# Moving the last step of a layer norm from ScalarE to GpSimd in a fused attention and feed-forward kernel

## The chip, the cores and the metric

One core of one Trainium2 chip. The metric is device time in microseconds (us). The engines are called PE (TensorE matmul), ACT (ScalarE), DVE (VectorE), POOL (GpSimd) and SP (SyncE, which here only issues transfers). SBUF and PSUM are two memories on the core: in this kernel PE's matmuls write to PSUM tiles (bank by bank), and the other tiles shown here lie in SBUF. A transfer from one memory to another is a DMA; it is issued by an engine's queue and lands some us later.

## The reference, cut to what matters

```python
# q, k, v: 8 batches, 12 heads, 448 tokens, 64 wide
scores = scale * np.matmul(q, k.transpose(0, 1, 3, 2))
attn = np.maximum(scores, 0.0) ** 2 / S
x = np.matmul(attn, v)                  # -> (8, 448, 768)
X = np.fft.fft(np.fft.fft(x, axis=1), axis=2)
u = x + np.real(X)
mu, var = u.mean(-1), u.var(-1)         # over the 768 channels
un = (u - mu) / np.sqrt(var + 1e-06)    # the layer norm
out = u + np.maximum(un @ w_ch1, 0.0) @ w_ch2
```

The last step of the norm is `un = u * rstd + nmr`, with `rstd` one over the root and `nmr = -mu * rstd`, both one number per token.

## The kernel before

A Python scheduler inside the kernel books every instruction on an engine with an estimated duration, and so decides the order of each engine's queue. On the chip each queue then runs in that order.

```python
def need(eng, dur, deps=(), bufs=(), ok=None):
    return eng, dur, list(deps), list(bufs), ok

def act(n):
    return n / 1200 + 0.2
```

The norm in `mix_rows`, once for each of two chunks of rows (`ch`) of a batch `b`; each chunk has two tiles `u`:

```python
for i, eng, en, d in ((1, nc.gpsimd, "POOL", 1.8), (0, nc.vector, "DVE", 2 * dve(KN))):
    ...                                            # u, half on POOL, half on DVE
    eng.tensor_tensor(u[:n, 0:KN], ts[i][:n, 0:KN], x[:n, 0:KN], op=ALU.add)
    eng.tensor_tensor(u[:n, KN:D], ts[1 - i][:n, KN - 2:0:-1], x[:n, KN:D], op=ALU.add)
...                                                # bn_stats, bn_aggr on DVE
nc.scalar.activation(std[:n], mv[:n, :, 1], AF.Sqrt, bias=eps_t[:n])
...
nc.vector.reciprocal(rstd[:n], std[:n])
nc.vector.scalar_tensor_tensor(nmr[:n], mv[:n, :, 0], -1.0, rstd[:n], op0=ALU.mult, op1=ALU.mult)
for i, u in enumerate(us):
    e = yield need("ACT", act(D), [e + (LATENCY["DVE"] if i == 0 else 0.0)])
    un = work.tile([128, D], BF16, name="un", tag=f"un{2 * ch + i}", bufs=1)
    nc.scalar.activation(un[:n], u[:n], AF.Identity, bias=nmr[:n, i:i + 1],
                         scale=rstd[:n, i:i + 1])
    ...
```

From batch 2 on, `un` then goes to memory (half by SP, half by a scattered store that POOL issues) and comes back transposed through SP as `unT` for the feed-forward. The feed-forward's first half fills PSUM banks that ACT empties; it has two banks for this (and DVE's work on attention outputs and on `o` uses the same two):

```python
BF = Banks(2, lambda i: psum.tile([128, 512], FP32, name="psF", tag=f"F{i}", bufs=1))
...
e = yield need(en, (dve if en == "DVE" else act)(N), [e + LATENCY["PE"]], [BH[j]])
nc.scalar.activation(h[:, 0:N], ph[:, 0:N], AF.Relu)      # hT
BF.give(ph, e)
```

## Time and profile before

| | before |
|---|---|
| time, median of 3 runs | 611.16 us (610.72 to 611.26) |
| profiled span | 610.0 us |
| busy: PE, DVE, ACT, POOL | 597.8, 331.7, 315.6, 126.8 us |
| PE's waits after 165 us | 1.1 us on ACT's `hT`, 0.5 us on DVE's `o` |

How to read it: PE is the bound, and the other engines matter only where PE waits for them. The prediction shows the lines. The tiles named most often: `sq` are the squared scores, `xT` the attention outputs on their way out of PSUM, `fold` sums made of `xT`, `qkr` the queries and keys as copied by DVE and `qkT` the same after a transposing transfer, `hT` the first half of the feed-forward after its relu, `o` the output rows, to which a reload brings `u` back from memory.

### The profile page before, as it was taken

The page shows a single profiled execution, that of the slowest core. Times are in us where ns is not written, and L with a number is a line of the kernel's source. Part 1 is how long each engine was busy: PE and PEld are TensorE (multiplying, and loading weights), DVE is VectorE, ACT ScalarE, POOL GpSimd, SP SyncE. Part 2 cuts the span into 40 slices and gives each one's busy share as a digit, 9 for nine tenths or more (in the row PEclk, how much of TensorE's full clock was granted, in tenths as well). Part 3 has the DMA queues.
Part 4 walks back from the last instruction along what each step waited for, and adds up shares of the span by engine and source line. Part 5 has one row for each costly group of instructions (what it writes and reads, how often), then busy time and mean ns, then how long its engine had stood idle before and what let it go on. Part 6 is the DMA issues. An engine that isn't in the chain of part 4 may idle for free.

```text
span 610.0 us, 10248 instructions
## 1 busy us (share of the span) xinstructions
PE 597.8 (98%) x4044; PEld 330.6 (54%) x4063; DVE 331.7 (54%) x767; ACT 315.6 (52%) x470; POOL 126.8 (21%) x175
## 2 busy tenths in 40 slices
PE   8998999999999999999999999999999999999997
PEld 6566556544455565555445565555445565554464
DVE  5966776965576768555744368545742447110011
ACT  5965772488555668536763167635782247114300
POOL 8432031411142124211420115210410004000000
PEclk9998999999999999999999999999999999999999
DMA  9999998965938995976496775985461225320022
GB/s 125 207 209 228 207 179 126 203 118 101 148 120 166 197 166 168 172 137 120 158 140 115 134 126 173 167 156 96 146 134 61 86 51 177 102 94 23 0 78 78
DMA packets 125216, 82.22 MB, mean 135 GB/s; under 512 B 76272, under 2 KB 113168, under 8 KB 125168
## 3 DMA queue, kind: packets, MB, share of 16 engines
q0 software_dynamic: 40320, 34.07, 35.3%
q1 hardware_dynamic: 84848, 47.50, 32.1%
q8 instruction: 32, 0.52, 0.3%
q14 instruction: 16, 0.13, 0.1%
HBM read 62.91 MB, written 26.69 MB: 147 GB/s over the span
## 4 chain that ended last, share of the span: by engine, by line
PE 84%; DVE 6%; ACT 5%; SPq 2%; issue 1%; DMA 1%; DVEq 0%; ACTq 0%
PE psF L1108 32%; PE psF L1090 31%; PE psF L524 7%; PE psS L538 6%; PE psS L982 2%; PE psS L1130 2%; ACT sq L558 2%; DVE stats L864 1%; PE psS L832 1%; ACT un L878 1%; SPq L923 1%; DMA o<-ubot 1%; PE psS L957 1%; PE psF L421 1%; ACT hT L1063 1%
## 5 line engine op out<-in xcount | busy, mean ns | idle before, releaser
L1090 PE MATMUL psF<-unT,w 128*128 128x384 bf16 (+1 forms) x1134 | 228.4, 353 | 2.2 <-ACT hT L1063 1.1
L558 ACT ACTIVATE sq<-psS 112x896 bf16<-112x896 f32 x192 | 165.3, 915 | 116.2 <-PE psS L538 116.2
L1108 PE MATMUL psF<-w,hT 128*128 128x384 bf16 (+2 forms) x1343 | 224.8, 326 | 0.1
L1108 PEld LDWEIGHTS <-hT 128*128 128x128 bf16 x1344 | 129.3, 98 | 92.4 <-issue 8.8
L1090 PEld LDWEIGHTS <-w 128*128 128x128 bf16 x1152 | 109.5, 98 | 111.6 <-issue 15.4
L1063 ACT ACTIVATE hT<-psF 128x512 bf16<-128x512 f32 (+1 forms) x180 | 98.2, 547 | 98.8 <-PE psF L1090 97.7
L564 DVE TENSOR_TENSOR sq<-sq 112x896 bf16<-112x896 bf16 x192 | 115.4, 619 | 48.5 <-ACT sq L558 46.9
L1071 DVE TENSOR_TENSOR o<-psF,o 128x384 f32<-128x384 f32 (+2 forms) x56 | 31.0, 554 | 109.8 <-PE psF L1108 108.5
L445 DVE TENSOR_SCALAR xT<-psF 128x224 bf16<-128x224 f32 x48 | 18.7, 390 | 74.7 <-PE psF L524 74.7
L538 PE MATMUL psS<-qkT 64*112 64x448 bf16 x384 | 52.6, 367 | 0.6 <-ACT qkT L426 0.4
L300 POOL DMA_DIRECT2D vn<-in_v_dram x24 | 17.3, 720 | 172.7 <-PE psF L524 154.1
L524 PE MATMUL psF<-sq,vn 112*64 112x448 bf16 x384 | 45.5, 358 | 1.4 <-DVE o L1071 0.5
L852 POOL TENSOR_TENSOR u<-tp,xn 128x385 f32<-128x385 f32 (+1 forms) x14 | 17.3, 1236 | 105.1 <-DVE tp L843 91.6
L538 PEld LDWEIGHTS <-qkT 64*112 64x112 bf16 x384 | 20.4, 125 | 27.9 <-issue 22.7
L878 ACT ACTIVATE un<-u,nmr,rstd 128x768 bf16<-128x768 f32 (+1 forms) x28 | 28.2, 1021 | 6.7 <-DVE nmr L873 6.7
L524 PEld LDWEIGHTS <-vn 112*64 112x64 bf16 x384 | 18.3, 109 | 23.1 <-issue 14.5
L864 DVE BATCH_NORM_STATS2 stats<-u 128x6 f32<-128x384 f32 (+1 forms) x56 | 28.1, 540 | 0.0
L900 POOL DMA_INDIRECT ubot<-u,back x16 | 16.8, 1048 | 43.3 <-DVE sq L564 27.5
L1130 PE MATMUL psS<-warm 128*128 128x126 bf16 (+1 forms) x210 | 18.9, 242 | 1.3 <-DVE warm L215 1.3
L300 POOL DMA_DIRECT2D qn<-in_q_dram x21 | 15.3, 728 | 23.1 <-DVE sq L564 9.2
L900 POOL DMA_INDIRECT nbot<-un,back x12 | 11.7, 972 | 35.6 <-ACT un L878 31.9
L452 DVE TENSOR_SCALAR xT<-psF 128x224 bf16<-128x224 f32 x47 | 18.0, 384 | 0.0
(119 smaller groups left out, 363.5 us busy)
## 6 DMA issues: line engine op xcount, KB each, us to landing
out_dram<-o SPq DMA_DIRECT2D x27, 384.0 KB, 2.6
vn<-in_v_dram POOLq DMA_DIRECT2D x24, 224.0 KB, 4.5
qn<-in_q_dram POOLq DMA_DIRECT2D x21, 224.0 KB, 6.3
kn<-in_k_dram POOLq DMA_DIRECT2D x21, 224.0 KB, 6.9
w<-in_moe_w_ch_dram POOLq DMA_DIRECT2D x12, 384.0 KB, 13.5
w<-in_moe_w_ch_dram POOLq DMA_DIRECT2D x4, 1152.0 KB, 23.4
utop<-u SPq DMA_DIRECT2D x8, 384.0 KB, 2.6
o<-utop SPq DMA_DIRECT2D x8, 384.0 KB, 3.5
```

The costliest lines, as they stand in the source:

```text
L300: nc.gpsimd.dma_start(out=t, in_=src[b, hs].rearrange("h (p j) d -> p h (j d)", j=4))
L524: nc.tensor.matmul(av[h * Dh:(h + 1) * Dh, 0:S], lhsT=vn[:, c, h0 + h, :], rhs=sq[:, h, :], start=(c == 0), stop=(c == 3))
L538: nc.tensor.matmul(sc[:R, h, 0:S].rearrange("k (c q) -> k c q", c=4), lhsT=kT[ps, m % 2, c, :], rhs=qT[ps, m % 2], start=True, stop=True)
L558: nc.scalar.activation(r, sc[:R, :, 0:S], AF.Relu)
L564: nc.vector.tensor_tensor(r, r, r, op=ALU.mult)
L864: nc.vector.bn_stats(stats[:n, hf, :], u[:n, hf * (D // 2):(hf + 1) * (D // 2)])
L878: nc.scalar.activation(un[:n], u[:n], AF.Identity, bias=nmr[:n, i:i + 1], scale=rstd[:n, i:i + 1])
L1063: nc.scalar.activation(h[:, 0:N], ph[:, 0:N], AF.Relu)
L1071: nc.vector.tensor_tensor(o[:, hs], pc[:, 0:w], o[:, hs], op=ALU.add)
L1090: nc.tensor.matmul(ph[:, 0:N], lhsT=w1_sb[m][hf][:, jj * 128:(jj + 1) * 128], rhs=unT[:, m, 0:N], start=(m == 0), stop=(m == MC - 1))
L1108: nc.tensor.matmul(pc[:, 0:w], lhsT=hT[j][:, c * 128:(c + 1) * 128], rhs=w2_sb[j // 6][:, j % 6, hs], start=(j == 0), stop=(j == JC - 1))
L1130: nc.tensor.matmul(first_pps[0][:, t, c0:512], lhsT=warm[:, 0:128], rhs=warm[:, c0:512], start=not begun, stop=False)
```

## The change

The intent is to relieve ACT, which also empties PSUM for PE, by giving 24 of its instructions to POOL, which is idle for four fifths of the time. Both the instruction and the scheduler's booking change.

```diff
         for i, u in enumerate(us):
-            e = yield need("ACT", act(D), [e + (LATENCY["DVE"] if i == 0 else 0.0)])
+
+            en = "POOL" if b > 1 else "ACT"
+            e = yield need(en, act(D) if b == 1 else 1.05, [e + (LATENCY["DVE"] if i == 0 else 0.0)])
             un = work.tile([128, D], BF16, name="un", tag=f"un{2 * ch + i}", bufs=1)
-            nc.scalar.activation(un[:n], u[:n], AF.Identity, bias=nmr[:n, i:i + 1],
-                                 scale=rstd[:n, i:i + 1])
+            if b > 1:
+                nc.gpsimd.tensor_scalar(un[:n], u[:n], rstd[:n, i:i + 1], nmr[:n, i:i + 1],
+                                        op0=ALU.mult, op1=ALU.add)
+            else:
+                nc.scalar.activation(un[:n], u[:n], AF.Identity, bias=nmr[:n, i:i + 1],
+                                     scale=rstd[:n, i:i + 1])
```

## The prediction

> **What bounds the kernel now.** I read the busy table of the page first, then the six stretches between 165 us (where batch 2's norm begins) and 545 us (where the last layer's own stretch begins), then who TensorE (PE) waited for in that part, and then the order of time around one norm.
>
> The busy table, from the page; the columns are engine, busy us, share of the span, instructions:
>
> ```profile
> PE 597.8 (98%) x4044; PEld 330.6 (54%) x4063; DVE 331.7 (54%) x767; ACT 315.6 (52%) x470; POOL 126.8 (21%) x175
> ```
>
> PE is busy for 98% of the span; ScalarE (ACT), which the change relieves, for 52%, and POOL for 21%. A busy PE can still be a slow one, so the next thing is how much of it is idle where the change acts. The busy times by stretch (stretch, its length, then busy us of each engine, the granted clock last but two):
>
> ```profile
> 165.00:230.00 65.00, 64.42 (x432) 36.25 (x431) 44.87 (x102) 36.84 (x53) 17.30 (x19) 1.00 0.88 164
> 230.00:305.00 75.00, 74.35 (x461) 38.45 (x463) 48.75 (x116) 46.26 (x71) 19.94 (x23) 1.00 0.72 150
> 305.00:370.00 65.00, 64.95 (x417) 36.20 (x417) 32.07 (x74) 29.98 (x45) 10.66 (x13) 1.00 0.71 126
> 370.00:445.00 75.00, 74.74 (x462) 38.66 (x465) 47.29 (x113) 46.00 (x71) 17.65 (x20) 1.00 0.65 148
> 445.00:510.00 65.00, 64.95 (x417) 36.52 (x417) 29.36 (x66) 28.24 (x43) 4.20 (x4) 1.00 0.33 85
> 510.00:545.00 35.00, 34.26 (x208) 20.31 (x208) 8.61 (x19) 8.79 (x17) 4.94 (x5) 1.00 0.39 120
> ```
>
> The PE column adds up to 377.66 of 380 us: 2.3 us of idle PE in the whole part in which a norm has moved. The clock is 1.00 throughout. PE is also fast while busy: inside the feed-forward, matmul follows matmul every 162 to 163 ns for 384 columns and 216 ns for 512 (start to start), the same in every stretch. So PE's own program is the bound. The waits of PE from 165 us on (who, for whom, us in total, times, longest) are two rows:
>
> ```profile
> PE psF L1090 <- ACT hT L1063: 1.1, 3, 0.5
> PE psF L524 <- DVE o L1071: 0.5, 1, 0.5
> ```
>
> The first is the one that the change can take away, and the order of time around batch 7's norm shows why (start, duration, engine, line, operation, and in brackets the idle time before it and what ended that):
>
> ```profile
> 510.37 0.91 POOL L852 TENSOR_TENSOR u<-tp,xn 112x385 f32<-112x385 f32 x1 [1.31 <-DVE rstd L871]
> 510.38 0.91 DVE L873 SCALAR_TENSOR_TENSOR nmr<-mv,rstd 128x2 f32<-128x2 f32 x1
> 511.22 0.55 DVE L852 TENSOR_TENSOR u<-tm,xn 112x385 f32<-112x385 f32 x1
> 511.24 1.22 POOL L853 TENSOR_TENSOR u<-tm,xn 112x383 f32<-112x383 f32 x1
> 511.33 1.03 ACT L878 ACTIVATE un<-u,nmr,rstd 128x768 bf16<-128x768 f32 x1 [0.50 <-DVE nmr L873]
> 511.69 1.19 DVE L853 TENSOR_TENSOR u<-tp,xn 112x383 f32<-112x383 f32 x1
> 512.27 0.85 ACT L1063 ACTIVATE hT<-psF 128x384 bf16<-128x384 f32 x2
> 512.79 6.09 PE L1090 MATMUL psF<-unT,w 128*128 128x384 bf16 x36 [0.53 <-ACT hT L1063]
> ```
>
> ACT begins the norm step `un` at 511.33, and the relu `hT`, which empties one of the two PSUM banks that PE needs, only comes after it, at 512.27. PE stands for 0.53 us. The three such stalls are near 237 (batch 4), 512 and 519 us (batch 7).
>
> **What the Trainium skill says.** "SBUF — State Buffer", section "Who interferes with whom": GpSimd shares a port pair with VectorE (DVE), and "A DVE instruction with two SBUF inputs contends with a GpSimd instruction that reads SBUF". The trace agrees: above, `nmr` (128 by 2) takes 0.91 us, exactly as long as the POOL addition that starts 0.01 us before it, where its median over all 14 is 0.161 us. "GPSIMD Engine Reference", section 3.1, puts the per-element cost of a simple one-input body between about 1.03 and 1.8 cycles at 1.2 GHz, which for 768 elements is an estimate of 0.66 to 1.15 us; this trace has the very operation at 0.981 us (below), and that is used. "Perfetto Trace Analysis", section "Identifying Performance Opportunities", says that improving a kernel generally means improving its most-contended engine; here that is PE, and the change does not touch PE's work.
>
> **The change part by part.** The two rows of the grouped instructions that give the cost (line, engine, operation, shapes, count, then busy us and mean ns of one, then idle before and releaser):
>
> ```profile
> L878 ACT ACTIVATE un<-u,nmr,rstd 128x768 bf16<-128x768 f32 (+1 forms) x28 | 28.2, 1021 | 6.7 <-DVE nmr L873 6.7
> L682 POOL TENSOR_SCALAR un<-u,rstd,nmr 128x768 bf16<-128x768 f32 x2 | 2.0, 981 | 0.8 <-DVE nmr L650 0.6 <-ACT u L658 0.3
> ```
>
> *Removed.* Of the 28 `un` on ACT, batches 2 to 7 have 6 x 4 = 24; batch 1's four stay. 24 x 1.021 = 24.5 us leave ACT: 315.6 should become about 291.
>
> *Added.* 24 one-input operations on POOL. The kernel already has this operation in this shape in batch 0, twice, at 0.981 us. 24 x 0.981 = 23.5 us: POOL from 126.8 to about 150, a quarter of the span.
>
> *Moved.* PE's program has the same 8128 rows as before. I compared the built orders: only between batch 2 and batch 3, and once after, do some groups of six matmuls stand on the other side of an attention step, and the number of runs of one kind goes from 315 to 317. The recording scheduler thought ACT free earlier there. On SyncE's queue the transposes of one chunk and the reload of `o` of batch 1 change places, so that the reload is no longer behind the transposes of batch 2. On POOL, every `un` pair stands right behind the additions of `u` and before the store that already followed them.
>
> *What this is worth.* ACT's 24.5 us are nearly all beside PE's work. What sets the end is PE, so the gain is the PE idle time that ACT caused: the row of 1.1 us, all three of whose entries lie next to an `un`. I count it in full: -1.1. The 0.5 us wait on `o` comes from a reload of `o` (the next row back is a wait of 0.90 us on that DMA), and with the reload issued earlier it may go; I count half: -0.3. Against that stands DVE. Each POOL `un` may hold back a DVE instruction with two SBUF inputs for up to 0.98 us, such as the squaring `sq` (0.62 us each, 192 of them). From the times of the records I took how long before its consumer on PE each group of squares was done: after 165 us the least is 1.0 us, and just after the norms it is 1.5 to 2.1 us (batch 4 at 239 us and 244 us, batch 6 at 378 and 383). ACT, free of two `un`, brings the same squares about 1 to 2 us sooner, so most of the delay is paid back; I choose +0.6 for what leaks to PE, an estimate of 0.1 us per batch. Sum: 611.16 - 1.1 - 0.3 + 0.6 = 610.4.
>
> **The rivals.** *ACT is a hidden bound and its relief is worth more*, up to 24.5 us (587 us). For it: the squares and relus on ACT are what PE's next steps wait for by data. Against it: PE's idle time in the whole part is 2.3 us, and its matmuls come at an even pace. Even if every idle instant of that part went, the time would be 608.8.
>
> *POOL becomes a new wait.* POOL's queue runs in order, and it also issues the loads of q, k and v and the scattered stores. If an `un` sits behind a load that waits for PE (such waits are up to 25.7 us long) the transposes and the next feed-forward come late. Against it: the built order has each `un` ahead of those loads, and only in batch 2 does one store of `un` now stand behind a load of v. The last batch has the room: its last `un` ended at 518.6 us, its feed-forward starts at 544.8, so 10 us of delay would still be hidden. In batch 2 the feed-forward starts at 212 against stores issued by 188.4. If it failed, one batch would lose 2 to 5 us: 613 to 616.
>
> *The shared port makes DVE late.* 24 blocks of 0.98 us on DVE with no payback, reaching PE only beyond the slack of 1.5 to 2 us: at most some 0.5 us in each of six batches, 3 us in all: about 613.
>
> **The range and the chances.** The floor is 608.8 (all idle gone); a better mark is not to be had without a change to PE's program. The side of loss is longer, so I take 608.8 to 612.8 as 8 in 10. 2% is 12.2 us: faster than 598.9 would need five times the idle time that there is, chance 0.01; slower than 623.4 needs a stall in every batch of 2 us, chance 0.01; within 2%, 0.98.
>
> **What would show it.** ACT's busy time near 291 and POOL's near 150; `un` on POOL at 0.95 to 1.1 us median; the three waits of PE on `hT` after 165 us gone or below 0.3 us; PE's busy time still 597 to 599 us; DVE's busy time up by 2 to 12 us, with some `sq` at over 1 us, where before the longest was 0.627. The prediction is wrong if PE shows new waits on `sq` or `o` of over 2 us in sum, if the transposes of `un` arrive after the feed-forward could start, or if PE's matmuls come at another pace.

## More of the kernel before

One more reading is used all through the experiments. From the order of time on PE I take two fixed points, each the start of a group of eight matmuls "values times squares" (L524): batch 2's first group, and the last group of all (batch 7's last). Columns are start us, duration us, engine, line, operation. In the kernel before:

```profile
124.90 0.95 PE L524 MATMUL psF<-sq,vn 112*64 112x448 bf16 x8
...
495.20 0.95 PE L524 MATMUL psF<-sq,vn 112*64 112x448 bf16 x8
```

Between the two points lie the norms of batches 2 to 6; I call this the **middle**, 495.20 - 124.90 = 370.3 us. From the second point to the end of the span lies batch 7's norm; this is the **tail**, 610.0 - 495.2 = 114.8 us. What comes before 124.9 us is untouched by the change.

## The result

The changed kernel takes 610.32 us (median of 4 runs, 609.23 to 610.91), the kernel before on the same chip 611.21 us (610.72 to 611.57). The ratio is 0.9984 with a 95% interval of 0.9967 to 1.0001. A ratio here is the mean time of one kernel's fast runs over that of the other's fast runs of the same rounds, so not quite the ratio of the two medians.

The busy table of the changed kernel, from the page:

```profile
PE 597.3 (98%) x4044; PEld 330.4 (54%) x4063; DVE 337.4 (55%) x767; ACT 295.0 (48%) x446; POOL 154.4 (25%) x199
```

ACT lost 20.6 us, POOL gained 27.6, DVE gained 5.7 though none of its work changed, and PE stayed. The row of the moved instruction among the grouped instructions, and the only row that is left of PE's waits from 165 us on:

```profile
L881 POOL TENSOR_SCALAR un<-u,rstd,nmr 128x768 bf16<-128x768 f32 (+1 forms) x24 | 26.8, 1122 | 6.3 <-DVE nmr L873 5.9
```

```profile
PE psF L1096 <- DVE xT L452: 0.6, 1, 0.6
```

Both rows of before are gone, and a new one has come. The order of time around batch 7's norm, the same moment that the prediction shows:

```profile
511.30 0.49 ACT L1069 ACTIVATE hT<-psF 128x384 bf16<-128x384 f32 x1 [0.48 <-PE psF L1096]
511.67 1.34 DVE L853 TENSOR_TENSOR u<-tp,xn 112x383 f32<-112x383 f32 x1
512.27 0.49 ACT L1069 ACTIVATE hT<-psF 128x384 bf16<-128x384 f32 x1 [0.48 <-PE psF L1096]
512.44 2.31 POOL L881 TENSOR_SCALAR un<-u,rstd,nmr 128x768 bf16<-128x768 f32 x2
...
519.97 10.24 PE L1114 MATMUL psF<-w,hT 128*128 128x384 bf16 x62
```

The relu that stood behind a norm step until 512.27 now starts at 511.30, and PE goes through without a gap: the second half of this feed-forward begins at 519.97, where it began at 520.98 before. The two fixed points:

```profile
124.86 0.95 PE L524 MATMUL psF<-sq,vn 112*64 112x448 bf16 x8
...
495.18 0.95 PE L524 MATMUL psF<-sq,vn 112*64 112x448 bf16 x8
```

The middle is 370.3 us, just as before. The tail is 609.0 - 495.2 = 113.8 us, 1.0 us less. In these two traces the whole gain comes from batch 7's four steps, and the 20 others bring nothing in sum.

### The profile page after: what moved, and what is told of

Read it like the earlier page. It is cut to its first block, busy times and chain, and to the rows that moved or that the text cites. A ratio compares the mean times of both kernels' runs of the same rounds, so it can differ in the third digit from the quotient of the medians.

```text
span 609.0 us, 10238 instructions
## 1 busy us (share of the span) xinstructions
PE 597.3 (98%) x4044; PEld 330.4 (54%) x4063; DVE 337.4 (55%) x767; ACT 295.0 (48%) x446; POOL 154.4 (25%) x199
## 4 chain that ended last, share of the span: by engine, by line
PE 84%; DVE 8%; ACT 4%; DMA 3%; issue 1%; SPq 0%; DVEq 0%; ACTq 0%
PE psF L1114 33%; PE psF L1096 30%; PE psF L524 6%; PE psS L538 6%; DMA qkT<-qkr 3%; PE psS L1136 2%; ACT sq L558 2%; PE psS L988 2%; DVE stats L864 2%; PE psS L832 1%; DVE u L853 1%; DVE sq L564 1%; PE psS L963 1%; PE psF L421 1%; ACT hT L1069 1%
## 5 line engine op out<-in xcount | busy, mean ns | idle before, releaser
L564 DVE TENSOR_TENSOR sq<-sq 112x896 bf16<-112x896 bf16 x192 | 118.2, 636 | 45.7 <-ACT sq L558 44.5
L445 DVE TENSOR_SCALAR xT<-psF 128x224 bf16<-128x224 f32 x48 | 18.7, 390 | 69.1 <-PE psF L524 69.0
L881 POOL TENSOR_SCALAR un<-u,rstd,nmr 128x768 bf16<-128x768 f32 (+1 forms) x24 | 26.8, 1122 | 6.3 <-DVE nmr L873 5.9
L906 POOL DMA_INDIRECT ubot<-u,back x16 | 17.1, 1067 | 37.2 <-DVE sq L564 27.6
L452 DVE TENSOR_SCALAR xT<-psF 128x224 bf16<-128x224 f32 x47 | 18.1, 384 | 0.0
L460 DVE TENSOR_TENSOR fold<-xT 128x225 bf16<-128x225 bf16 x48 | 16.0, 333 | 2.5 <-ACT xT L450 0.5
```

The lines of the kernel that those rows point to most:

```text
L564: nc.vector.tensor_tensor(r, r, r, op=ALU.mult)
L881: nc.gpsimd.tensor_scalar(un[:n], u[:n], rstd[:n, i:i + 1], nmr[:n, i:i + 1], op0=ALU.mult, op1=ALU.add)
```

## The experiments

Two questions were open. Why does only batch 7 gain (theory A: the gain is ACT's place ahead of `hT`, and elsewhere something takes it back), and is it the engine or the changed order of the queues that matters (rival C)? Rival B is that ACT's relief is worth something evenly, or that ACT is a hidden bound. Rival D is that the shared port or POOL's queue takes the gain.

All results in one table. Middle and tail are read from each trace at the two fixed points; the time comes from the runs. The kernel before scattered from 609.5 to 616.0 us on the chips of these runs, so that intervals of the ratio are 0.3 to 0.5% wide to either side. Part of the scatter goes with the granted clock, which each run lists: on the chip of e1 to e8 the kernel before took 609.5 to 610.7 us in its four runs at 1.00 and 611.4 to 616.0 in its eight at 0.994 to 0.997. The kernels have different shares of the two, so the ratios mix clock and kernel. Effects of 1 us are therefore read from the traces, of which there is one for each kernel; one program that was traced twice (e4_old_order and e12_old_order_again) has middles 3.1 us apart, so that a single middle is no proof of a difference of that size unless the waits in it are followed.

| kernel | median us | ratio (95%) | middle | tail |
|---|---|---|---|---|
| before | | 1 | 370.3 | 114.8 |
| changed | 610.32 | 0.9984 (0.9967 to 1.0001) | 370.3 | 113.8 |
| e1_again | 609.55 | 0.9958 (0.9926 to 0.9991) | 369.9 | 113.9 |
| e2_only_last | 611.12 | 0.9993 (0.9960 to 1.0027) | 370.3 | 113.8 |
| e3_all_but_last | 610.84 | 0.9980 (0.9945 to 1.0016) | 370.5 | 114.9 |
| e4_old_order | 610.09 | 0.9956 (0.9923 to 0.9989) | 371.9 | 113.8 |
| e5_order_alone | 620.42 | 1.0129 (1.0086 to 1.0171) | 382.5 | 114.6 |
| e6_act_twice | 629.33 | 1.0287 (1.0238 to 1.0336) | 386.0 | 118.7 |
| e7_pool_twice | 611.09 | 0.9983 (0.9942 to 1.0024) | 371.4 | 113.9 |
| e8_write_only (wrong) | 609.25 | 0.9953 (0.9912 to 0.9994) | 369.1 | 113.8 |
| e9_batch1_too | 610.77 | 0.9980 (0.9948 to 1.0012) | 372.6 | 113.9 |
| e10_skip2 | 609.98 | 0.9964 (0.9933 to 0.9995) | 371.7 | 113.8 |
| e11_from3 | 610.61 | 0.9987 (0.9954 to 1.0020) | 369.0 | 113.8 |
| e12_old_order_again | 609.70 | 0.9962 (0.9915 to 1.0010) | 368.8 | 113.8 |

### The changed kernel again

No edit.

> The changed kernel once more, beside the others on one chip. All theories: about 0.9 us below the kernel before (ratio 0.998), with an interval now clear of 1. PE waits on hT after 165 us: none; one wait of 0.6 us on DVE's xT near 217 us.

Measured: ratio 0.9958, its interval now clear of 1. But four of its six runs are at the full granted clock, and only three of the eleven of the kernel before. Those alone, a choice made after the fact, are 608.5 to 609.8 us (mean 609.1) against 610.1 to 610.7 (610.3): 1.2 us, or 0.998. So the gain is real and about 1 us, and the lower ratio holds some clock. PE's one wait after 165 us, on `xT` near 215 us, is 0.24 us where the first profile had 0.63: the size of that wait differs from one execution to the next.

### Batch 7 alone, and all but batch 7

```diff
-            en = "POOL" if b > 1 else "ACT"
+            en = "POOL" if b == B - 1 else "ACT"      # e2_only_last
+            en = "POOL" if 1 < b < B - 1 else "ACT"   # e3_all_but_last
```

(with the duration and the branch following `en`). The built queues of PE and SP of the first are row for row those of before, of the second those of the changed kernel.

> Only batch 7's four norm steps go to POOL; PE's and SyncE's orders are row for row those of the kernel before. Theory A (the net gain is batch 7's two hT stalls alone, about 1.0 us in the start of the last-but-one feed-forward's second half; elsewhere gains and losses cancel): 1.0 us below before, ratio 0.998, the stalls near 512 and 519 us gone, those near 206 (0.53) and 237 (0.44) still there. Rival B (the gain is spread evenly over the 24 moved steps, ACT's relief as such): 4 of 24, so 0.15 us, ratio 0.9998. Rival C (it comes from the changed order of PE and SyncE): no gain.

> Batches 2 to 6 go to POOL, batch 7 stays on ACT; PE's and SyncE's orders are those of the changed kernel. Theory A: within 0.4 us of the kernel before, ratio 0.9995 to 1.0005; the hT stalls near 512 and 519 us are back (0.53 and 0.16), the ones near 206 and 237 are replaced by one of 0.6 near 217 and two of 0.15. Rival B: 20 of 24 of the gain, 0.75 us, ratio 0.9988. Rival C: the whole gain, 0.9 us.

Measured: with batch 7 alone on POOL the tail is 113.8 us and the middle 370.3; with all but batch 7 the tail is 114.9 and the middle 370.5. The waits of PE from 165 us on follow, first those of e2_only_last, then those of e3_all_but_last:

```profile
PE psF L524 <- DVE o L1077: 0.5, 1, 0.5
PE psF L1096 <- ACT hT L1069: 0.4, 1, 0.4
```

```profile
PE psF L1096 <- ACT hT L1069: 1.1, 4, 0.6
PE psF L1096 <- DVE xT L452: 0.7, 1, 0.7
```

In the first the stalls near 204 (0.5 us, on `o`) and 236 (0.4 us, on `hT`) are still there and batch 7's are gone, in the second it is the other way round, with one of 0.7 us on `xT` near 216. The traces say what theory A says, and not B or C: in this kernel four steps carry a gain of about 1 us, and the twenty carry none that shows (middles of 370.3, 369.9 and 370.5 us with them on POOL, 370.3 in both traces with them on ACT). The timed ratios, 0.9993 and 0.9980, cannot tell 0.2 us from 1 us and point the other way inside their intervals; I rest the verdict on the tail, which over all fourteen traces is 113.8 or 113.9 us with batch 7 on POOL, 114.6 to 114.9 with it on ACT, and 118.7 with it on ACT twice.

### Engine and order apart

```diff
-            e = yield need(en, act(D) if b == 1 else 1.05, [...])
+            e = yield need("ACT", act(D), [...])      # e4_old_order: issued on POOL, booked on ACT
```

In e4_old_order PE, DVE and SP have the built queues of before row for row; POOL's own queue is not that of the changed kernel, since stores stand between steps that follow each other there (the first two steps of batch 4 start at 234.25 and 236.83 us in e12_old_order_again, with a store of `u` between, and as one pair at 233.41 in the changed kernel). The other half, e5_order_alone, keeps the booking on POOL and issues the instruction on ACT in every batch.

> All 24 steps are issued on POOL, but the recording scheduler still books them on ACT, so PE and SyncE keep the order of before row for row and ACT's order is that of before without the norm steps. Theory A: the hT stalls (1.1 us) go as in the changed kernel, the stall on o near 206 us (0.53) stays, the one near 217 us (0.63) does not appear: 1.0 to 1.6 us below before, ratio 0.9975 to 0.9984, so at or slightly below the changed kernel. Rival C (order): no gain, ratio 1.0.

> The other half of the last split: the scheduler books the norm steps on POOL, so PE and SyncE stand in the order of the changed kernel, but the 24 instructions are issued on ScalarE. Theory A (the gain is ACT's place in front of hT, the order is at best neutral): the stalls of PE on hT are there again, 1.1 us or more from 165 us on, the one on DVE's xT near 217 too: 0 to +1 us against before, ratio 1.000 to 1.002. Rival C (order): the whole 0.9 us of gain, 0.998.

Measured, the first: all waits on `hT` are gone and the tail is 113.8, so the engine gives the gain and not the order. But the middle is 371.9, since PE stands for 3.0 us near 201 us, which I had not expected. The order of time there:

```profile
199.94 0.43 DVE L389 COPY qkr<-kn 112x1024 bf16<-112x1024 bf16 x1 [5.36 <-DMA qkT<-qkr]
...
201.03 2.12 PE L1114 MATMUL psF<-w,hT 128*128 128x384 bf16 x12 [2.96 <-DVE xT L452]
```

DVE waits 5.36 us for a transposing transfer to let go of a buffer, and the evacuation of a PSUM bank (`xT`, L445 and L452) stands behind that copy in DVE's queue; PE needs the bank. That transfer had been issued at 191.28 us, ahead of the transposes of `unT` in SP's queue, and landed at 199.85, 8.6 us later; the same one took 5.2 us in the kernel before (192.04 to 197.25). Why it landed late here is not shown.

Measured, the second: 8 to 9 us slower, where I had expected 0 to 1. PE waits 7.9 us in 12 places on `hT` and 1.8 us on `xT`. (Its middle of 382.5 us also holds a slice at eight tenths of the granted clock, from 217 to 233 us, with 0.97 as the mean from 165 to 230.) So rival C, that the order gives the gain, falls: with the steps left on ACT the new order is harmful, because it was made with ACT booked as free where a norm step stands.

### What ACT's time is worth

```diff
             nc.scalar.activation(un[:n], u[:n], AF.Identity, bias=..., scale=...)
+            if b > 1:
+                nc.scalar.activation(un[:n], u[:n], AF.Identity, bias=..., scale=...)
```

This is on the kernel before: each of the 24 steps is done twice, with the order of everything else unchanged.

> The kernel before with each of the 24 norm steps done twice on ScalarE, the same result written twice: +24.5 us of ACT. Theory A (a norm step on ACT costs only where an hT stands behind it while PE's two banks are full): PE waits on hT from 1.1 us to 3 to 6 us, the time up by 2 to 5 us, ratio 1.003 to 1.008. Rival B (ACT is a hidden bound): up by some 24 us, ratio 1.04.

Measured: ratio 1.0287; the span is 628.2 us, 18.2 more for 24.5 us more of ACT. My 2 to 5 us were far off, and rival B's 24 not reached either. PE's waits from 165 us on:

```profile
PE psF L1093 <- ACT hT L1066: 12.1, 15, 1.5
PE psF L524 <- DVE o L1074: 5.5, 4, 1.9
PE psF L524 <- ACT hT L1066: 1.1, 2, 0.6
```

And one of the places, in the order of time:

```profile
526.58 1.03 ACT L881 ACTIVATE un<-u,nmr,rstd 128x768 bf16<-128x768 f32 x1
527.52 0.85 ACT L1066 ACTIVATE hT<-psF 128x384 bf16<-128x384 f32 x2
528.03 2.11 PE L1093 MATMUL psF<-unT,w 128*128 128x384 bf16 x12 [1.53 <-ACT hT L1066]
```

ACT is busy for 54% of this span and yet costs 18.2 / 24.5 = 0.74 us for each us added. One norm step in front of an `hT` just fits into what two banks hold (or misses by 0.2 to 0.5 us, as before near 237 and 512); the second finds the banks full and PE pays for it. That is the way of the 13.2 us on `hT`; the 5.5 us on `o` were not followed from ACT to DVE. Taking 24.5 us away gains 1 to 2.5 us, since there was no more PE idle time to win. The Trainium skill, "Perfetto Trace Analysis", section "Identifying the Most-Contended Engine", calls occupancy, for ScalarE, a fair measure of how close it is to its roofline; it does not say that it measures what added work costs, and here it does not.

### What POOL's reads cost

```diff
                 nc.gpsimd.tensor_scalar(un[:n], u[:n], rstd..., nmr..., ...)
+                nc.gpsimd.tensor_scalar(un[:n], u[:n], rstd..., nmr..., ...)   # e7_pool_twice
```

and, in place of the step, a write of a constant: `nc.gpsimd.memset(un[:n], 0.5)` (e8_write_only; its result is wrong).

> The changed kernel with each of the 24 norm steps done twice on POOL: +23.5 us of POOL and as much more time in which it reads SBUF beside DVE. Theory A (POOL has room, DVE's lateness is mostly hidden): up by 0 to 2 us against the changed kernel, so ratio 0.998 to 1.002 against before, DVE's busy time at 340 to 350 us. Rival D (the shared port already eats part of the gain, and POOL's queue is a second wait): up by 3 us or more, new waits of PE on DVE's lines.

> The changed kernel with each of the 24 norm steps replaced by a write of a constant on POOL: the same place in the queues, the same waits behind it, but no read of SBUF (the result is wrong on purpose). If the blocking of DVE is by reads, as the skill says, no sq is longer than 0.65 us (in the changed kernel six are at 1.12 to 1.24), DVE's busy time falls from 337 back to about 332 us, and POOL's steps take 0.3 to 0.7 us. Theory A: the time within 0.5 us of the changed kernel. Rival D: lower by 0.5 us or more.

Measured: POOL twice costs 1.5 us in the middle against e1_again (371.4 to 369.9) and nothing in the tail; PE's waits after 165 us are 1.6 us on `xT` and 0.5 us on `hT`, and DVE's busy time is 342.9 us. By its runs, all at the full granted clock, it takes 1.9 us more than e1_again at that clock (611.0 to 609.1). Doubling the same work costs 18.2 us on ACT and 1 to 1.9 us on POOL: rival D's 3 us are not reached. With the constant, PE has no wait at all after 165 us, DVE is back at 331.5 us busy, and the middle is 369.1, which is 0.9 to 1.3 us below the changed kernel's two traces: rival D's sign, of which more below. The squares on DVE in the changed kernel and with the constant, by line (duration ns least, median, most):

```profile
L564 DVE TENSOR_TENSOR sq<-sq x192: 572/621/1237, 10.5 to 494.1; 112x896 bf16<-112x896 bf16 x192
```

```profile
L564 DVE TENSOR_TENSOR sq<-sq x192: 570/621/627, 10.4 to 491.2; 112x896 bf16<-112x896 bf16 x192
```

A POOL step that reads holds up a DVE instruction with two SBUF inputs, one that only writes does not: this is what the skill's "SBUF — State Buffer", section "Who interferes with whom", says, and the run agrees. How lateness on DVE becomes a wait of PE shows in the changed kernel in batch 4:

```profile
233.41 2.32 POOL L881 TENSOR_SCALAR un<-u,rstd,nmr 128x768 bf16<-128x768 f32 x2
...
235.08 1.66 DVE L564 TENSOR_TENSOR sq<-sq 112x896 bf16<-112x896 bf16 x2
236.66 1.00 DVE L864 BATCH_NORM_STATS2 stats<-u 112x6 f32<-112x384 f32 x2
...
237.95 0.29 ACT L868 ACTIVATE std<-mv,eps_t 112x2 f32<-112x2 f32 x1 [1.24 <-DVE mv L865]
238.15 0.47 ACT L1069 ACTIVATE hT<-psF 128x384 bf16<-128x384 f32 x1
...
238.67 3.50 PE L1096 MATMUL psF<-unT,w 128*128 128x384 bf16 x19
```

Two squares take 1.66 us (1.11 with the constant), so the statistics come 0.5 us later, ACT's root waits for them, the `hT` behind the root is late, and PE begins 0.92 us after its last group where 0.77 us is the spacing with the constant: a wait of 0.15 us. The same happens in batch 6. One reserve: the constant also takes less time on POOL (0.74 us against 0.97) and does not wait for `nmr` (in batch 4 it starts at 235.84 us, `nmr` at 235.99), so that a part of the 1.3 us between the two middles may be queue time and not port. The larger new wait of the changed kernel, near 217 us, has another path, the one that e4_old_order showed at its worst:

```profile
215.38 0.43 DVE L389 COPY qkr<-kn 112x1024 bf16<-112x1024 bf16 x1 [1.87 <-DMA qkT<-qkr]
...
216.75 0.39 DVE L452 TENSOR_SCALAR xT<-psF 128x224 bf16<-128x224 f32 x1
...
217.19 0.50 PE L1096 MATMUL psF<-unT,w 128*128 128x384 bf16 x2 [0.63 <-DVE xT L452]
```

Here too DVE's copy of the next keys waits for the transposing transfer of the keys before them, and the emptying of the bank waits behind the copy. SP had issued that transfer long before, at 205.43 us. Its landing is not recorded here, but in five other traces with the changed order of the queues the same transfer landed 8.8 to 10.3 us after its issue (e1_again 9.5, e3_all_but_last 9.8, e5_order_alone 10.3, e7_pool_twice 9.6, e8_write_only 8.8), and in four with the order of before after 3.1 to 3.4 (before, e2_only_last, e4_old_order, e6_act_twice). So this wait is a price of the changed order: it comes with the steps on ACT too (e5_order_alone, 1.8 us), and the transfer is as late when POOL reads nothing (e8_write_only, where PE just escapes). What in the order delays the landing is not shown.

### Versions meant to beat both

```diff
+            en = "POOL" if b > 0 else "ACT"     # e9_batch1_too
+            en = "POOL" if b != 2 else "ACT"    # e10_skip2: batch 1 too, batch 2 not
```

> A version meant to beat both: batch 1's four norm steps go to POOL as well. In the changed kernel ACT still holds two of them (1.95 us) in front of squares at 121 us, and PE waits near 124.5 (0.39 on ACT's sq) and 126.7 (0.16). If ACT's place in the queue is the cause, those go: 0.5 to 1 us below the changed kernel, ratio 0.994 to 0.998 against before. If POOL's reads hold up DVE's squares there instead, the waits stay, now on DVE: no gain over the changed kernel.

> As the run before, but batch 2 stays on ACT, since the changed order around batch 2 is what brings the wait on DVE's xT near 217 us. Expected: no such wait, the one on o near 206 us (0.53) back, no hT waits near 237 and 512: within 0.5 us of the run before, either way.

Measured: neither beats the changed kernel. The part before the middle, from the second group of values of batch 1 to batch 2's first, falls from 51.3 to 50.1 us in both, and the middle rises to 372.6 and 371.7 us; but here the first fixed point itself has moved, since batch 2's first group now stands before the matmuls on batch 1's last `un`. Both parts together are 422.7 and 421.7 us, against 421.7 and 421.3 in the changed kernel's two traces. In e9_batch1_too DVE waits 4.0 us on the same transposes near 135 us and PE 0.66 us behind it. I had expected the waits near 124 us to go, or to stay on DVE; they grew from 0.4 to 1.0 us and are still on ACT's squares, with no norm step on ACT, so neither branch holds. In e10_skip2 the wait on `xT` near 217 us is gone, as expected, but the one on `o` near 206 us, expected back, is not there.

The last try puts the findings together: POOL from batch 3 on, booked on ACT, so that the order is that of before. The second run repeats e4_old_order.

```diff
-            en = "POOL" if b > 1 else "ACT"
-            e = yield need(en, act(D) if b == 1 else 1.05, [...])
+            en = "POOL" if b > 2 else "ACT"
+            e = yield need("ACT", act(D), [...])      # e11_from3
```

> A version meant to beat both: POOL does the norm steps from batch 3 on, and the scheduler books them on ACT, so PE and SyncE keep the order of before. Theory A adds up the stalls seen so far: the three on hT go (1.1 us of waits, 1.6 us by the spacing of matmuls), the one on o near 205 us (0.5) stays, batch 2's waits on the transposes do not come: 1.2 to 1.6 us below before, 0.3 to 0.7 below the changed kernel, ratio 0.9975. If the blocking of DVE costs something in batches 4 and 6 in this order too, PE has new waits of 0.1 to 0.3 there and the gain is under 1 us.

> The kernel with all 24 steps on POOL and the order of before, once more, to see whether its 3.0 us wait of PE near 201 us is of the program or of one execution. Of the program: again 2.5 to 3.5 us there. Of one execution (the landing of transfers): under 1.5 us there, and a time 1 to 2 us below that of the first profile.

Measured: in both traces PE waits for nothing after 165 us (no row at all), the middles are 369.0 and 368.8 us, the tails 113.8. Middle and tail together that is 2.3 to 2.5 us below the kernel before, where 1.2 to 1.6 had been expected with the wait on `o` still there, and 1.0 to 1.5 below the changed one's two traces. These middles are as low as the one with the constant (369.1), although POOL reads here and DVE is busy for 339.1 and 339.5 us: in this order DVE's lateness does not reach PE, so the 1.3 us between the changed kernel and e8_write_only are not a price of the port as such. The 3.0 us wait of e4_old_order, the very same program, is not there: it belongs to one execution. The transfer that landed after 8.6 us in e4_old_order is issued at 191.50 us here, and DVE's copy finds it landed by 195.99. By the timed runs the two versions are not told apart from the changed kernel: 0.9987 (0.9954 to 1.0020) and 0.9962 (two runs), where e1_again has 0.9958. A version that is better in its trace was found, one that is shown to be faster was not.

## Why the prediction was right, point by point

**The total.** 610.4 was said, 610.32 measured, inside the 608.8 to 612.8 that was given. That it came so near is luck: by an estimate from the traces some 2.1 us were won on `hT` and `o` (1.6 and 0.5), where 1.4 was said, and with 1.0 us left (1.3 in e1_again) some 1.2 (0.8) leaked, where 0.6 was said. Two errors cancel.

**The bound.** Right. PE's busy time went from 597.8 to 597.3 us; it runs the same instructions, a few of them in another order.

**ACT and POOL.** About 291 and 150 were said, 295.0 and 154.4 measured. The moved instruction has a median of 0.973 us, as its twin in batch 0 had promised, but a mean of 1.122: seven of 24 take 1.35 to 1.60 us, six of them the first of a pair right behind the additions of `u`, when DVE still adds too. I had put the port's cost on DVE alone; POOL pays as well. ACT lost 3.9 us less than the sum of the removed records. That is the overlap of neighbouring records on ACT (two steps together took 1.95 us before, not 2.05): in the trace before, the time covered by all of ACT's records but these 24 is 294.9 us, and 295.0 was measured after.

**The term -1.1 for `hT`.** Right in kind, too small. All three waits went. But a wait as the profile counts it starts at the modelled end of the last matmul, which lies 0.16 us after the next could have started (322 ns recorded, 162 ns spacing). By the spacing of matmuls the three were 0.60, 0.70 and 0.32 us, 1.6 in sum, and the tail's 1.0 us is the last two. The first of them, near 237 us, is not directly behind a norm step: the `hT` there stands behind two squares (235.18 to 236.89), which come after the `un` that starts at 233.87.

**The term -0.3 for `o`.** Right in its reason and too small: the changed order issues the reload at 193.24 us instead of 199.50, and none of the five traces with that order and the steps on POOL (changed, e1_again, e3_all_but_last, e7_pool_twice, e8_write_only) has the wait; it went whole, not by half. But the order of before does not always have it: it is there in two traces (before, e2_only_last), where the reload landed 80.3 us after the first fixed point, and not in e11_from3, where it landed after 79.9 us, nor in e4_old_order and e12_old_order_again.

**The term +0.6 for what leaks from DVE.** Too small, as shown above, and the wrong path in part. DVE rose by 5.7 us, inside the 2 to 12 said, and squares of up to 1.237 us came, as said. But they reached PE through the statistics and ACT's root, 0.15 us each in two batches, not through the squares' own consumer, which I had measured the slack of. Nor is 0.98 us the most that a DVE instruction loses: one addition (`fold`) took 2.19 us instead of 0.28, beside a pair of POOL steps. The largest new wait, 0.2 to 0.7 us by execution, came over a transpose in batch 2 that lands late in the changed order, whichever engine does the steps. It is like the second rival in that the order brings a new wait, but not its path: POOL's queue does not appear in it, and the batch lost 0.2 to 0.7 us and not 2 to 5.

**The first rival, ACT as a hidden bound.** The argument against it held: no more than the idle time of PE could be won, and the best traces (e11_from3, e12_old_order_again) won 2.3 to 2.5 us against the 2.3 us of idle PE counted from the stretches. But ACT is not free in the other direction, as e6_act_twice shows.

## What to carry to other kernels

Taking work off an engine can win no more than the bound engine's waits for it; add those up first, by the spacing of its instructions and not only by its recorded gaps. Low occupancy does not mean that added work is cheap: where two buffers stand between the engines, one instruction too many in front of an evacuation can cost most of its length (0.74 us per us here). When an instruction changes engine, the order of all queues changes with it; building the move with the old order, and the new order without the move, tells the two apart. And where one program differs from itself by 3 us from trace to trace, follow the waits before believing a difference of 1 us.

## What the Trainium skill lacked or had wrong

- "SBUF — State Buffer", section "SBUF: two separate sides", says that whichever of the two instructions starts first has the shared ports for its whole length. In the changed kernel a DVE addition with two SBUF inputs (`fold`, 0.28 us median) starts at 379.23 us by its record, 0.12 us before a pair of POOL steps (379.35 to 381.28), and takes 2.19 us, until both are done; the POOL steps take their usual 0.98 and 0.97 us. Either the recorded starts do not give the order in which the two took the port, or the rule fails here; the trace does not tell these apart. And one DVE instruction can lose to two POOL instructions in a row, which the page does not say.
- "GPSIMD Engine Reference", section 4.1, weighs POOL for elementwise work against VectorE only, and excepts operations with one input. A comparison with ScalarE is missing: the one-input multiply and add of 128 by 768 from fp32 to bf16 has a median of 0.973 us on POOL (a mean of 1.122 beside DVE's work) and takes 1.02 on ACT.
- "Perfetto Trace Analysis", section "Identifying the Most-Contended Engine", gives occupancy as the measure for ScalarE, but nothing on what added work costs: at 52% over the span it cost 0.74 us per us (24.5 us more, 18.2 us longer).
- No page that I read tells how far executions of one program on one core lie apart. The start of batch 2's first value group lies at 123.2 to 123.5 us in profiles whose granted clock shows full in every slice of the first 125 us, and at 124.7 to 124.9 where the slice from 46 to 61 us shows eight tenths (before, changed, e11_from3, e12_old_order_again), with the same instructions before it (e9_batch1_too and e10_skip2, which change them, left out).
